# Low parts of weights and of gates made on GpSimd while the weights are decoded

## The chip, the cores and the metric

The kernel runs on one core of a Trainium2 chip. Its time is the device time of one execution in microseconds. TensorE is called PE here, VectorE DVE, ScalarE ACT, GpSimd POOL and SyncE SP, as in the profile.

## The reference

Four sequences of 768 tokens go through banded attention with eight heads, and the result through a layer of two matrix products with a gate between them:

```python
scores = scale * np.matmul(q, k.transpose(0, 1, 3, 2))   # then a bias by distance and a mask
a = np.exp(scores - max); a = a / (sum(a) + 1e-09)
x = np.matmul(a, v)                      # 3072 tokens x 512
h = x @ w_in                             # 512 -> 2048
g = h * np.clip(h + 3.0, 0.0, 6.0) / 6.0
out = g @ w_out                          # 2048 -> 512
```

The two weight matrices reach the kernel as 64-bit floats, seen as pairs of 32-bit words.

## The kernel before

The 3072 tokens are eight blocks of 384. For each block the kernel computes attention for four pairs of heads (which gives x) and then the two products. The 2048 inner columns are 16 *slices* of 128. For one slice `first` gives PE 12 matmuls of 384 columns into a bank hp, `gate` makes g from it (ACT, L185, then DVE, L186), and `second` gives PE 9 matmuls of 512 columns that add the slice's share to three banks acc. Each operand is split into a high part, rounded to the format that PE multiplies, and a low part, the rest; three of the four products of parts are added. So there are xh and xl, w1h and w1l, w2h and w2l, gh and gl. `high` makes gh, and `rest` makes gl = g - gh on DVE (L199), for which g has one buffer (`gp1`), gh four and gl three.

The weights come in 32 chunks of 128 x 512, w1 and w2 of a slice in turn, and `decode` makes them into 32-bit floats, high and low. For one chunk: SP loads the words (wst, three buffers); ACT takes the magnitude of the high word (wz, two buffers, L410) and makes the last places from the low word (we, L422; for the first six chunks POOL does this, L415); DVE clamps wz (L444) and shifts it (L445), puts the sign and exponent back (L453) and adds we (L457); ACT rounds to the high part (L461); and DVE subtracts to get the low part (L450), after which wz is free again.

The kernel begins with attention for the first nine pairs; the first three slices of block 0 lie beside it. Then come 21 *common slices*: block 0 (its remaining 13) and block 1 (its first 8) take turns as the digits of ORDER say, while the decode goes on beside them. Block 0 is the first to use a chunk throughout. After that the other slices of block 1 and all of blocks 2 to 7 run beside the attention of the block that follows. (At the end a flag chooses between storing the last block and a general path for other masks, which isn't taken here.)

`halves` lays out the common slices. For a slice it puts down `first`, the gate, gh (on ACT here) and gl, and then, with `finish`, the second product of the slice before. So a gl is used about one slice after its own gate.

How much of the decode is put between two slices is set by a plan when the program is written. `work(pe, dve)` adds the estimated costs of what was just put down to two sums, and as long as the sum of DVE is behind that of PE, `decode_step` takes the next quarter of a chunk from `decode`, which yields its estimated DVE cost: 0.68 for L444 and L445 of chunk i, 0.6 for the low part of chunk i-1, 0.6 for L453 of chunk i and 0.69 for L457. A slice counts 4.2 for PE (2.1 for each product) and 0.94 for DVE (0.47 for the gate, 0.47 for gl). `decoded_to` draws more steps where PE needs a chunk.

PE, POOL and SP work through their instructions in the order in which they are written (`in_order`). DVE and ACT get an order from the scheduler, which starts from the written one. Each engine serves its queue strictly in its order, and an instruction that waits holds up all that is behind it.

Of the kernel before, what the change touches and what calls it, by code (L numbers as in the profile page):

```python
# [9 lines left out]
F32 = mybir.dt.float32  # L10
# [4 lines left out]
ALU = mybir.AluOpType  # L15
# [38 lines left out]
WAKE = 9  # L54
FIRST = 3
CROWDED = 6
ORDER = "101001010010010100100"

def store(nc, pool, out, row, acc, last=False):
# [6 lines left out]
class Kernel:  # L66
# [127 lines left out]
            self.nc.scalar.copy(out=gh, in_=g)  # L194
        return gh

    def rest(self, g, gh):
        gl = self.lp.tile([P, TB], F32R, name="gl")
        self.nc.vector.tensor_tensor(out=gl, in0=g, in1=gh.bitcast(F32), op=ALU.subtract)  # L199
        return gl  # L200

    def second(self, f, acc, gh, gl, tiles=range(NT)):
# [201 lines left out]
    def magnitude(self, i):  # L404
# [6 lines left out]
        if i == 0:  # L411
            self.tc.add_manual_dep(self.nc.cur_bb.bb.instructions[-1], self.held, mybir.DependencyInfo(
                mybir.DependencyClass.NoSync, mybir.DependencyReason.DATA), reason="behind the first pairs")
        if i < CROWDED:
            self.nc.gpsimd.tensor_scalar(out=self.e[i], in0=words[:, :, 0].bitcast(U32), scalar1=2.0 ** -29, scalar2=0.0,  # L415
                                         op0=ALU.mult, op1=ALU.add)

    def last_places(self, i):
        if CROWDED <= i < 2 * NF:
            words = self.raw[i].rearrange("p (c w) -> p c w", w=2)  # L420
            before = self.nc.cur_bb.bb.instructions[-1].name
            self.nc.scalar.mul(out=self.e[i], in_=words[:, :, 0].bitcast(U32), mul=2.0 ** -29)  # L422
            self.tc.add_manual_dep(self.nc.cur_bb.bb.instructions[-1], before, mybir.DependencyInfo(
                mybir.DependencyClass.NoSync, mybir.DependencyReason.DATA), reason="behind the high part")
# [5 lines left out]
    def decode(self):  # L430

        nc = self.nc
        ts, stt, tt = nc.vector.tensor_scalar, nc.vector.scalar_tensor_tensor, nc.vector.tensor_tensor
        N = 2 * NF
        self.magnitude(0)
        for i in range(N + 1):
            a, b = i < N, i > 0
            if a:  # L440
                if i + 2 < N:
                    self.fetch(i + 2)
                z = self.z[i]
                ts(out=z.bitcast(F32), in0=z.bitcast(F32), scalar1=LEAST, scalar2=MOST, op0=ALU.max, op1=ALU.min)  # L444
                ts(out=z, in0=z, scalar1=0x07FFFFFF, scalar2=3, op0=ALU.bitwise_and, op1=ALU.logical_shift_left)  # L445
            yield 0.68 * a
            if b:
                hi, sh = self.part(i - 1, self.w1h, self.w2h)
                lo, _ = self.part(i - 1, self.w1l, self.w2l)
                tt(out=lo, in0=sh(self.z.pop(i - 1).bitcast(F32)), in1=hi.bitcast(F32), op=ALU.subtract)  # L450
            yield 0.6 * b
            if a:
                stt(out=z, in0=self.raw[i].rearrange("p (c w) -> p c w", w=2)[:, :, 1], scalar=-0x40000000, in1=z,  # L453
                    op0=ALU.bitwise_and, op1=ALU.bitwise_or)
            yield 0.6 * a
            if a:
                tt(out=z, in0=z, in1=self.e.pop(i), op=ALU.add)  # L457
                if i + 1 < N:
                    self.magnitude(i + 1)
                hi, sh = self.part(i, self.w1h, self.w2h)  # L460
                nc.scalar.copy(out=hi, in_=sh(z.bitcast(F32)))  # L461
                self.last_places(i + 1)
            yield 0.69 * a
# [16 lines left out]
        while self.decoded < 4 * (i + 1) + (2 if i < 2 * NF - 1 else 4):  # L480
            self.decode_step()

    def halves(self, steps, pool=False):


        for block, f, x, acc in steps:
            self.decoded_to(2 * f)
            g = self.gate(self.first(f, x), block == len(self.blocks) - 1 and f == NF - 1)
            gh = self.high(g, pool) if pool else None
            self.work(2.1, 0.47)  # L490
            yield
            if not pool:
                gh = self.high(g, pool)
            gl = self.rest(g, gh)
            self.work(0, 0.47)
            if self.last is not None:
                self.finish()
                yield
            self.last = (block, f, acc, gh, gl)
# [46 lines left out]
    def banded(self, flag):  # L546
# [12 lines left out]
        with ExitStack() as early, ExitStack() as words:  # L559
            x0 = self.x_tiles(self.pool("x0", 1, ctx=early, side="right"))  # L560
            xs = [x0, self.x_tiles(), self.x_tiles()]
            self.decoding(words, 3, 2, side="right")
            self.decoding_steps = self.decode()

            self.decoded_all = words.close
            self.fetch(0)
            self.given[1] = LEAD
            self.allowed = 4 * NF + 3
            acc = []
            with ExitStack() as ctx:  # L570
                self.load(2, False)
                self.fetch(1)
                for n in range(2):
                    self.load(n, True)
                self.plain_distances(ctx)
                self.attending(ctx, 9, 5)
                pairs = [Pair(self, n, xs[n // NPAIR], True) for n in range(EARLY)]
                todo = self.halves([(0, f, xs[0], acc) for f in range(FIRST)])

                def half():  # L580
                    if self.stage == "both":
                        next(todo, None)

                for n in range(-2, EARLY + 1):
                    if n + 2 < NPAIR:
                        self.distances(n + 2)
                    if n + 2 == EARLY:
                        self.stage = "both"
                        acc.extend(self.acc_tiles())
                    if n + 2 < EARLY:  # L590
                        weigh = []
                        for t in range(NT):
                            weigh.append(pairs[n + 2].scores(t))
                            if n == 0 and t < NT - 1:
                                self.spin(2)
                        if n < 0:
                            self.spin(5)
                        self.load_next(n + 2, False)
                        self.work(1.440, 0)
                    for t in range(NT):  # L600
                        if n + 2 < EARLY:
                            weigh[t]()
                            self.work(0, 0.64)
                            if t == NT - 1 and n == -2:
                                self.load(2, True)
                        if 0 <= n < EARLY:
                            pairs[n].turn(t)
                            if n == 0 and t < NT - 1:
                                self.spin(3)
                            self.work(0.396, 0)  # L610
                        if n + 1 in (0, 1):
                            pairs[n + 1].sum_up(t)
                            pairs[n + 1].normalize(t)
                        if t == 0:
                            if 2 <= n + 1 < EARLY:
                                pairs[n + 1].sum_up()
                            half()
                        if t == 1:
                            if n > 0:
                                pairs[n - 1].values()  # L620
                                self.work(1.350, 0.47)
                            if 2 <= n + 1 < EARLY:
                                for u in range(NT):
                                    pairs[n + 1].normalize(u)
                        if t == 2:
                            half()
                for _ in todo:
                    pass
            self.weights()
            self.packed_masks()  # L630
            self.allowed = 4 * (2 * NF + 1)
            acc1 = [pool.tile([P, BANK], F32, name=name) for pool, name in ((self.ps_s, "sp"), (self.ps_t, "tp"), (self.ps_x, "xp"))]
            self.given[1] = max(self.given)
            next_f, todo = [FIRST, 0], []
            for block in map(int, ORDER):
                todo.append((block, next_f[block], xs[block], (acc, acc1)[block]))
                next_f[block] += 1
            for _ in self.halves(todo):
                pass
            self.decoded_to(2 * NF - 1)  # L640
        self.attending(self.ctx, 3, 2, side="right")
# [13 lines left out]
        for i in range(2, len(self.blocks)):  # L655
# [7 lines left out]
            steps = [(i, f, x, acc) for f in range(NF)]  # L663
# [386 lines left out]
```

## Time and profile before

| | us |
|---|---|
| median of 3 runs (653.16 to 655.09) | 655.08 |
| the profiled execution | 654.68 |
| its span in the trace | 652.9 |
| PE busy in the span | 639.4 |
| DVE busy | 356.9 |
| ACT busy | 257.4 |
| POOL busy | 167.6 |

Times in the trace count from the start of the span. A group's row gives line, engine, operation, output and inputs with their shapes, how often it occurs, its busy time and the mean of one in ns, and behind the last bar the engine's idle time just before it and what ended most of that. In a timeline row the first two numbers are start and duration in us. Durations of one engine's neighbours overlap at their ends, so an engine's busy time is less than their sum. A row by stages gives the stretch, its length, the busy time of each engine, PE's granted clock, the share of the DMA engines and their GB/s.

### The profile page before, as it was taken

The numbers are of one execution on the slowest core, as the hardware profiler recorded it, in microseconds if no ns is written. First come the engines' busy times: TensorE is split into PE (matmuls) and PEld (weight loads), VectorE is DVE, ScalarE is ACT, GpSimd is POOL, SyncE is SP. The second block draws the span as 40 slices with busy tenths as digits, with TensorE's granted clock in tenths as the row PEclk, the third lists the DMA queues.
The fourth block names the chain that finished last, engine by engine and source line by source line (L and its number), as shares of the span: only waits on it lengthen the run. The fifth ranks groups of instructions, "written<-read, shape, count | busy, mean of one in ns | idle before, by whom it ended". The sixth has DMA issues, their size and how long they took to land.

```text
span 652.9 us, 13102 instructions
## 1 busy us (share of the span) xinstructions
PE 639.4 (98%) x4761; PEld 564.1 (86%) x4761; DVE 356.9 (55%) x1066; ACT 257.4 (39%) x706; POOL 167.6 (26%) x372
## 2 busy tenths in 40 slices
PE   8989999999999999999999999999999999999997
PEld 7778999997888889988898888888898888989985
DVE  5889999995644554255444454345542554422222
ACT  6897777775423222242313232132222423121111
POOL 5667000001422322034122332123220341202100
PEclk9999999999999999999999999999999999999999
DMA  7675644443565564346553455525643454310001
GB/s 281 182 238 194 189 157 149 143 129 113 126 189 169 147 192 125 90 118 165 164 134 102 117 154 163 141 78 154 184 126 89 122 136 122 94 43 8 1 0 54
DMA packets 47122, 86.23 MB, mean 132 GB/s; under 512 B 6504, under 2 KB 28872, under 8 KB 47048
## 3 DMA queue, kind: packets, MB, share of 16 engines
q1 hardware_dynamic: 46760, 85.03, 44.4%
q8 instruction: 40, 0.66, 0.4%
q14 instruction: 34, 0.28, 0.1%
q10 hardware_dynamic: 288, 0.26, 0.1%
HBM read 60.30 MB, written 24.97 MB: 131 GB/s over the span
## 4 chain that ended last, share of the span: by engine, by line
PE 83%; DVE 6%; ACT 4%; DMA 2%; POOL 2%; issue 2%; SPq 1%; POOLq 0%; ACTq 0%
PE hp L174 38%; PE acc L206 35%; ACT n L895 3%; PE xp L971 3%; PE sp L862 2%; PE sp L971 2%; DMA there<-blocks 1%; POOL n L915 1%; SPq L953 1%; DVE n L891 1%; PE xp L206 1%; PE tp L206 1%; PE sp L206 1%; DVE blocks L937 1%; DVE wz L453 1%
## 5 line engine op out<-in xcount | busy, mean ns | idle before, releaser
L185 ACT ACTIVATE g<-hp,small 128x384 f32<-128x384 f32 x127 | 73.6, 580 | 277.6 <-PE hp L174 173.4
L174 PE MATMUL hp<-xh,w1h 128*128 128x384 f32 x512 | 173.8, 340 | 0.5 <-ACT w1h L461 0.5
L174 PE MATMUL hp<-xh,w1l 128*128 128x384 f32 x512 | 172.3, 337 | 0.5 <-DVE w1l L450 0.5
L174 PE MATMUL hp<-xl,w1h 128*128 128x384 f32 x512 | 171.7, 335 | 0.0
L192 POOL TENSOR_SCALAR gh<-g 128x384 fp32r<-128x384 f32 x104 | 53.6, 515 | 343.6 <-DVE g L186 320.7
L186 DVE SCALAR_TENSOR_TENSOR g<-g,hp 128x384 f32<-128x384 f32 x128 | 70.7, 553 | 123.3 <-ACT g L185 122.1
L206 PE MATMUL acc<-w2h,gh 128*128 128x512 f32 x336 | 133.2, 396 | 0.0
L206 PE MATMUL acc<-w2h,gl 128*128 128x512 f32 x336 | 131.7, 392 | 0.0
L206 PE MATMUL acc<-w2l,gh 128*128 128x512 f32 x336 | 131.6, 392 | 0.0
L199 DVE TENSOR_TENSOR gl<-g,gh 128x384 fp32r<-128x384 f32 x128 | 71.5, 559 | 70.7 <-POOL gh L192 58.3
L895 ACT ACTIVATE n<-n,least 128x136 f32<-128x136 f32 (+2 forms) x192 | 79.5, 415 | 65.5 <-DVE least L891 64.8
L174 PEld LDWEIGHTS hp<-xh,w1h 128*128 128x128 f32 x512 | 96.1, 188 | 6.5 <-issue 3.1
L174 PEld LDWEIGHTS hp<-xl,w1h 128*128 128x128 f32 x512 | 96.2, 188 | 2.5
L174 PEld LDWEIGHTS hp<-xh,w1l 128*128 128x128 f32 x512 | 96.1, 188 | 1.1 <-DVE w1l L450 0.8
L915 POOL TENSOR_SCALAR n<-n,sums 128x136 f32<-128x136 f32 (+2 forms) x186 | 81.8, 457 | 38.3 <-DVE sums L906 23.1
L206 PEld LDWEIGHTS acc<-w2h,gh 128*128 128x128 f32 x336 | 63.1, 188 | 15.2 <-issue 3.3
L206 PEld LDWEIGHTS acc<-w2h,gl 128*128 128x128 f32 x336 | 63.1, 188 | 13.7 <-DVE gl L199 0.3
L206 PEld LDWEIGHTS acc<-w2l,gh 128*128 128x128 f32 x336 | 63.1, 188 | 11.4
L937 DVE STREAM_TRANSPOSE blocks<-n 128x256 f32<-128x256 f32 x138 | 51.1, 423 | 25.3 <-POOL n L915 20.8
L895 ACT ACTIVATION_READ_ACCUMULATOR n<-n,least 128x1 f32 x192 | 35.9, 187 | 0.0
L891 DVE CUSTOM_DVE_ANT_0 n<-sp,dl 128x136 f32<-128x136 f32 x60 | 17.7, 295 | 14.7 <-PE tp L862 14.7
L410 ACT ACTIVATE wz<-wst 128x512 f32<-128x512 f32 x32 | 21.5, 674 | 5.7 <-DVE w2l L450 2.8
(119 smaller groups left out, 644.6 us busy)
## 6 DMA issues: line engine op xcount, KB each, us to landing
there<-blocks SPq DMA_DIRECT2D x92, 192.0 KB
wst<-w SPq DMA_DIRECT2D x32, 512.0 KB
weights<-there SPq DMA_DIRECT2D x161, 96.0 KB
load<-pairs SPq DMA_DIRECT2D x31, 444.0 KB
load<-pairs SPq DMA_DIRECT2D x32, 384.0 KB
out<-o SPq DMA_DIRECT2D x23, 256.0 KB
weights<-there SPq DMA_DIRECT2D x23, 24.0 KB
there<-blocks SPq DMA_DIRECT2D x4, 72.0 KB
```

The lines of the kernel that those rows point to most:

```text
L174: self.nc.tensor.matmul(hp, lhsT=self.w1(w, f)[:, kt, :], rhs=a[:, kt, :], start=(n == 0), stop=(n == 3 * NKT - 1))
L185: nc.scalar.activation(out=g, in_=hp, func=AF.Relu, bias=self.three, scale=1.0)
L186: nc.vector.scalar_tensor_tensor(out=g, in0=g, scalar=6.0, in1=hp, op0=ALU.min, op1=ALU.mult)
L192: self.nc.gpsimd.tensor_scalar(out=gh, in0=g, scalar1=1.0, scalar2=0.0, op0=ALU.mult, op1=ALU.add)
L199: self.nc.vector.tensor_tensor(out=gl, in0=g, in1=gh.bitcast(F32), op=ALU.subtract)
L206: self.nc.tensor.matmul(acc[tt], lhsT=a[:, tk], rhs=self.w2(w, f), start=(f == 0 and j == 0), stop=(f == NF - 1 and j == 2))
L410: self.nc.scalar.activation(out=self.z[i].bitcast(F32), in_=words[:, :, 1].bitcast(F32), func=AF.Abs)
L891: nc.vector.tensor_tensor_reduce(out=e[:, j, lo:end], in0=sp[j][:, lo:end], in1=d, op0=ALU.add, op1=ALU.min, scale=scale, scalar=3.0e38, a ...
L895: nc.scalar.activation(out=e[:, j, lo:end], in_=e[:, j, lo:end], func=AF.Exp, bias=self.least[:, i:i + 1], scale=-1.0, accum_out=self.sums ...
L915: nc.gpsimd.tensor_scalar(out=e[:, j, lo:end], in0=e[:, j, lo:end], scalar1=over, scalar2=0.0, op0=ALU.mult, op1=ALU.add)
L937: nc.vector.transpose(out=self.blocks[:, :, s, t].rearrange("p b j q -> p j b q"), in_=e[:, :, c:c + P].rearrange("p j (b q) -> p j b q", ...
L971: nc.tensor.matmul(xps[j * D:(j + 1) * D, t * P:(t + 1) * P], lhsT=vt[0:K, t, j * D:(j + 1) * D], rhs=self.part(t, j, c, K), start=(c == 0 ...
```

## The change

Two kinds of subtractions move from DVE to POOL: the low part of weights of every chunk from the seventh on (26 of 32), and gl of the 21 common slices. Their costs in the plan become 0: the quarter with the low part yields 0 from `i = 7` on, and `work` is called with 0 instead of 0.47 after gl. POOL serves its queue in the written order.

```diff
+QUIET = 6
...
-    def rest(self, g, gh):
+    def rest(self, g, gh, pool=False):
         gl = self.lp.tile([P, TB], F32R, name="gl")
-        self.nc.vector.tensor_tensor(out=gl, in0=g, in1=gh.bitcast(F32), op=ALU.subtract)
+        (self.nc.gpsimd if pool else self.nc.vector).tensor_tensor(out=gl, in0=g, in1=gh.bitcast(F32), op=ALU.subtract)
...
-                tt(out=lo, in0=sh(self.z.pop(i - 1).bitcast(F32)), in1=hi.bitcast(F32), op=ALU.subtract)
-            yield 0.6 * b
+                (nc.gpsimd if i > QUIET else nc.vector).tensor_tensor(out=lo, in0=sh(self.z.pop(i - 1).bitcast(F32)),
+                                                                      in1=hi.bitcast(F32), op=ALU.subtract)
+            yield 0.6 * b * (i <= QUIET)
...
-    def halves(self, steps, pool=False):
+    def halves(self, steps, pool=False, low=False):
...
-            gl = self.rest(g, gh)
-            self.work(0, 0.47)
+            gl = self.rest(g, gh, low)
+            self.work(0, 0 if low else 0.47)
...
-            for _ in self.halves(todo):
+            for _ in self.halves(todo, low=True):
```

The plan's costs decide what lies between two slices, so the order of DVE, ACT and POOL changes; that of PE and of SP does not. On DVE, between the gates of the sixth and the seventh common slice (L186 g before, L187 after; wz is the chunk being decoded, w2l a low part), there stood:

```order
245 L186 SCALAR_TENSOR_TENSOR g<-g,hp 128x384
246 L445 TENSOR_SCALAR wz<-wz 128x512
247 L450 TENSOR_TENSOR w2l_147<-wz,w2h_146 128x512
248 L453 SCALAR_TENSOR_TENSOR wz<-wst,wz 128x512
249 L199 TENSOR_TENSOR gl<-g,gh 128x384
250 L457 ISA wz<-wz,we 128x1024
251 L444 TENSOR_SCALAR wz<-wz 128x512
252 L445 TENSOR_SCALAR wz<-wz 128x512
253 L186 SCALAR_TENSOR_TENSOR g<-g,hp 128x384
```

Now there stands between the same two gates, with line numbers one or two higher:

```order
238 L187 SCALAR_TENSOR_TENSOR g<-g,hp 128x384
239 L459 ISA wz<-wz,we 128x1024
240 L445 TENSOR_SCALAR wz<-wz 128x512
241 L446 TENSOR_SCALAR wz<-wz 128x512
242 L455 SCALAR_TENSOR_TENSOR wz<-wst,wz 128x512
243 L459 ISA wz<-wz,we 128x1024
244 L445 TENSOR_SCALAR wz<-wz 128x512
245 L446 TENSOR_SCALAR wz<-wz 128x512
246 L455 SCALAR_TENSOR_TENSOR wz<-wst,wz 128x512
247 L187 SCALAR_TENSOR_TENSOR g<-g,hp 128x384
```

The low part of weights and gl are gone, and instead of five decode operations there are eight, those of two chunks.

On POOL, behind the last masks that are prepared for later attention (dl) and ahead of what the second attention stage needs (blocks, load), there stood nothing:

```order
45 L298 TENSOR_SCALAR dl<-d_85 32x128
46 L298 TENSOR_SCALAR dl<-d_86 32x136
47 L306 MEMSET blocks 128x3x192
48 L848 TENSOR_SCALAR load_72<-load_72,over 128x384
49 L192 TENSOR_SCALAR gh<-g 128x384
```

Now the queue goes on at that place as follows:

```order
45 L299 TENSOR_SCALAR dl<-d_85 32x128
46 L299 TENSOR_SCALAR dl<-d_86 32x136
47 L200 TENSOR_TENSOR gl<-g,gh 128x384
48 L451 TENSOR_TENSOR w1l_145<-wz,w1h_144 128x4x128
49 L451 TENSOR_TENSOR w2l_147<-wz,w2h_146 128x512
50 L200 TENSOR_TENSOR gl<-g,gh 128x384
51 L451 TENSOR_TENSOR w1l_145<-wz,w1h_144 128x4x128
52 L451 TENSOR_TENSOR w2l_147<-wz,w2h_146 128x512
53 L200 TENSOR_TENSOR gl<-g,gh 128x384
```

Two low parts of weights lie between two gl. The end of this piece of the queue is

```order
84 L451 TENSOR_TENSOR w1l_1025<-wz,w1h_1024 128x4x128
85 L200 TENSOR_TENSOR gl<-g,gh 128x384
86 L451 TENSOR_TENSOR w2l_1027<-wz,w2h_1026 128x512
87 L200 TENSOR_TENSOR gl<-g,gh 128x384 x7
88 L307 MEMSET blocks 128x3x192
```

so that the last low part stands between the fourteenth and the fifteenth gl, and seven gl follow it; blocks and what is behind it come after all of them.

## The prediction

> **What bounds the kernel now.** I read the page's busy shares and slices first, then the busy times of the stretch that the change touches, then PE's timeline there, and then the groups of that stretch by shape.
>
> ```profile
> PE 639.4 (98%) x4761; PEld 564.1 (86%) x4761; DVE 356.9 (55%) x1066; ACT 257.4 (39%) x706; POOL 167.6 (26%) x372
> ## 2 busy tenths in 40 slices
> PE   8989999999999999999999999999999999999997
> DVE  5889999995644554255444454345542554422222
> ACT  6897777775423222242313232132222423121111
> POOL 5667000001422322034122332123220341202100
> ```
>
> The span is 652.9 us, and PE is busy in 98% of it, so whatever does not make PE wait is free, and whatever does is paid in full. One of these slices is 16.3 us. From the fifth to the tenth DVE stands at 9 while POOL stands at 0: that is the stretch of the common slices, in which the weights are decoded beside the first two blocks, and the change moves work there from the one engine to the other.
>
> ```profile
> 64.00:146.00 82.00, 82.00 (x425) 74.51 (x422) 78.98 (x160) 62.96 (x111) 0.00 (x0) 1.00 0.49 153
> 146.00:160.00 14.00, 13.04 (x106) 10.80 (x106) 8.28 (x19) 7.21 (x13) 2.65 (x4) 1.00 0.25 70
> ...
> 149.04 0.44 PE L174 MATMUL hp<-xh,w1h 128*128 128x384 f32 x1 [0.47 <-ACT w1h L461]
> 150.13 0.44 PE L174 MATMUL hp<-xh,w1l 128*128 128x384 f32 x1 [0.48 <-DVE w1l L450]
> ```
>
> The columns are PE, PEld, DVE, ACT and POOL busy. DVE works 78.98 of 82.00 us, yet PE loses nothing before 146. It waits twice, 0.47 and 0.48 us, where the last hidden slice's weights come late. So a relieved DVE can give back 0.95 us here and no more: this bounds the gain.
>
> **The change, part by part.** These are the groups of the same 82 us by shape, first DVE's.
>
> ```profile
> L453 DVE SCALAR_TENSOR_TENSOR wz<-wst,wz 128x512 int32<-128x512 int32 x24 | 16.5, 686 | 0.0
> L457 DVE CUSTOM_DVE_ANT_0 wz<-wz,we 128x1024 uint16<-128x1024 uint16 x24 | 16.5, 686 | 0.4
> L199 DVE TENSOR_TENSOR gl<-g,gh 128x384 fp32r<-128x384 f32 x20 | 11.1, 553 | 0.0
> L186 DVE SCALAR_TENSOR_TENSOR g<-g,hp 128x384 f32<-128x384 f32 x19 | 10.5, 551 | 2.4 <-ACT g L185 2.2
> L445 DVE TENSOR_SCALAR wz<-wz 128x512 int32<-128x512 int32 x24 | 10.1, 423 | 0.2
> L444 DVE TENSOR_SCALAR wz<-wz 128x512 f32<-128x512 f32 x24 | 10.1, 421 | 0.0
> L450 DVE TENSOR_TENSOR w1l<-wz,w1h 128x512 fp32r<-128x512 f32 x12 | 8.2, 686 | 0.0
> L450 DVE TENSOR_TENSOR w2l<-wz,w2h 128x512 fp32r<-128x512 f32 x12 | 8.2, 686 | 0.0
> L161 DVE TENSOR_TENSOR xl<-xp,xh 128x384 fp32r<-128x384 f32 x1 | 0.5, 545 | 0.0
> ```
>
> *What leaves DVE.* The busy times add up to 91.7 us against the 78.98 of the whole engine: neighbours overlap at their ends, and a duration counts for 0.861 of itself. A chunk without its low part is 421 + 423 + 686 + 686 = 2216 ns, so 1.91 us of DVE; a gate (L186) is 0.47 us; each low part of weights that leaves frees 0.59, each gl 0.48.
>
> *What POOL pays.* The trace has no large two-input operation on POOL. The nearest rows are these.
>
> ```profile
> L192 POOL TENSOR_SCALAR gh<-g 128x384 fp32r<-128x384 f32 x104 | 53.6, 515 | 343.6 <-DVE g L186 320.7 <-PE acc L206 16.5 <-ACT xh L160 4.0
> L1034 POOL MEMSET const-float32-0.0<- 128x1 f32 x1 | 0.1, 100 | 0.2 <-issue 0.2
> ...
> 54.20 0.66 POOL L415 TENSOR_SCALAR we<-wst 128x512 int32<-128x512 uint32 x1
> 55.54 1.00 POOL L415 TENSOR_SCALAR we<-wst 128x512 int32<-128x512 uint32 x1 [0.68 <-DVE wz L453]
> ...
> 54.26 1.14 DVE L453 SCALAR_TENSOR_TENSOR wz<-wst,wz 128x512 int32<-128x512 int32 x1
> 55.93 1.15 DVE L457 CUSTOM_DVE_ANT_0 wz<-wz,we 128x1024 uint16<-128x1024 uint16 x1
> ```
>
> With one input POOL takes 0.66 us for 512 columns and 0.52 for 384, of which 0.10 is there with one column. That is the lower end. Two inputs read one after the other double what is left: 0.10 + 2 x 0.56 = 1.21 us and 0.10 + 2 x 0.415 = 0.93 us, the upper end. I take the upper, because 1.1 ns per column and input is what POOL's rows show at both widths, and nothing in them suggests a second input for free. [...]
>
> *What the two engines do to each other.* The last four rows decide the forecast. L453 needs 0.69 us when POOL is idle. Beside the POOL operation of 54.20 to 54.86 it takes 1.14 and ends 0.54 us after POOL does. L457 beside 55.54 to 56.54 takes 1.15 and ends again 0.54 us after; and that POOL operation itself took 1.00, not 0.66, because it began while L453 still ran. So these DVE operations and POOL's take turns. By the rows, time on POOL is time taken from DVE, and the move brings no parallel work except beside the gate, which reads one of its inputs from the matmul's banks. [...]
>
> *What the order does.* The planner now counts nothing on DVE for the moved work, so each slice draws two chunks where it drew one or two (1.9 against 1.3 by its own costs). The rows of the change's section show two full decodes between two gates on DVE, and a gl, two low parts, a gl on POOL. All queues are served in order. So a gl, for which PE waits, now stands behind two low parts on POOL; its gate stands behind two decodes on DVE; the next slice's ACT operation waits for gl, since g has one buffer; and a chunk's first step waits for the low part two chunks before, since wz has two. The order of PE and of SP's transfers stays as it was.
>
> ```profile
> 70.25 0.55 DVE L199 TENSOR_TENSOR gl<-g,gh 128x384 fp32r<-128x384 f32 x1
> ...
> 123.56 0.56 DVE L199 TENSOR_TENSOR gl<-g,gh 128x384 fp32r<-128x384 f32 x1
> ...
> 125.87 0.39 PE L206 MATMUL sp<-w2h,gl 128*128 128x512 f32 x1
> ```
>
> *The sum.* POOL's queue now has 13 gl and 25 low parts from the first common slice's gl up to the fourteenth's; then one low part and seven gl are left. Before, these two gl start at 70.25 and 123.56: 53.3 us, 4.1 us a slice. In turns, the same stretch costs
>
> - DVE: 25 chunks x 1.91 = 47.7 us
> - POOL, low parts of weights: 25 x 1.21 = 30.3 us
> - POOL, gl: 13 x 0.93 = 12.1 us
> - the gates, 13 x 0.47 = 6.1 us, half of them beside POOL: 3.1 us
>
> together 93.2 us, 7.2 a slice, 39.9 more than before. PE takes the fourteenth gl at 125.87, 1.75 us after it is made (124.12), so the first 1.75 us are hidden; and the 0.95 us of late weights go, because the decode now ends seven slices early. Net: 39.9 - 1.75 - 0.95 = 37.2 us. From the fifteenth slice on PE runs at its old pace, as all that follows does: it is only shifted. The profiled execution took 654.68 us (span 652.9 and 1.8 around it), the median of the three timed runs is 655.08, within 0.1%. Forecast: 654.7 + 37.2 = 692 us. Its own range: 0.54 instead of 0.59 us a turn for the long DVE operations, and likewise the short ones, takes off 25 x 0.17 = 4 us; gates wholly hidden or not at all, 3 either way: 685 to 695, and up to 698 where handing over costs 0.1 us for some 30 turns.
>
> **The rivals.**
>
> *Turns and chain together (slower still).* With two wz buffers, a chunk's steps follow each other at their full durations, 2.22 instead of 1.91 us, and nothing hides the gate (0.55): 25 x (2.22 + 1.21) + 13 x (0.93 + 0.55) = 104.9 us, net +48.9, so 704 us. For it: DVE's order has the four steps of a chunk in a row. Against it: POOL can use the gaps. PE could reach the same place by its clock:
>
> ```profile
> 32.00:48.00 16.00, 13.29 (x139) 11.13 (x138) 14.21 (x59) 15.23 (x51) 10.22 (x21) 1.00 0.71 230
> ...
> 44.31 0.44 PE L971 MATMUL xp<-pt,load 128*64 128x128 f32 x4 [1.42 <-issue]
> ```
>
> PE waits 1.42 us here, more than anywhere between the first pairs and the end, with the granted clock at 1.00 (the column after POOL's); the forecast has about 3 us a slice. At half clock a slice would need 8.2 us, more than 7.2: 13 x 8.2 - 53.3 - 2.7 = +50.6, 705 us. [...]
>
> *POOL cheap.* A two-input operation costs what one input does: 47.7 + 25 x 0.66 + 13 x 0.52 + 3.1 = 74.1 us, net +18.1: 673 us. For it: only that the trace has no such row. Against it: 1.1 ns per column at both widths.
>
> *Side by side (not slower).* POOL's two-input operations do not take turns with DVE's. Then POOL needs 2 x 1.21 + 0.93 = 3.35 us a slice, less than PE's 4.1; DVE needs 47.7 + 6.1 = 53.8 us for the stretch, as PE's 53.3; and the next limit is ACT:
>
> ```profile
> L422 ACT ACTIVATE we<-wst 128x512 int32<-128x512 uint32 x24 | 16.2, 674 | 0.0
> L410 ACT ACTIVATE wz<-wst 128x512 f32<-128x512 f32 x23 | 15.5, 673 | 3.5 <-DVE w1l L450 1.6 <-DVE w2l L450 1.2
> L185 ACT ACTIVATE g<-hp,small 128x384 f32<-128x384 f32 x19 | 11.0, 580 | 8.5 <-PE hp L174 7.4 <-DVE wz L457 0.9
> L194 ACT CAST gh<-g 128x384 fp32r<-128x384 f32 x20 | 10.2, 511 | 2.2 <-DVE g L186 1.8
> L461 ACT CAST w2h<-wz 128x512 fp32r<-128x512 f32 x12 | 7.5, 623 | 3.5 <-DVE wz L457 3.0
> L461 ACT CAST w1h<-wz 128x512 fp32r<-128x512 f32 x12 | 7.4, 621 | 1.3 <-DVE wz L457 0.6
> L160 ACT CAST xh<-xp 128x384 fp32r<-128x384 f32 x1 | 0.5, 472 | 0.0
> ```
>
> These add up to 68.3 us against 62.96 busy, a factor of 0.92. 25 chunks at (674 + 673 + 623) x 0.92 = 1.81 us and 13 gates at (580 + 511) x 0.92 = 1.00 us make 58.3, net 58.3 - 53.3 - 2.7 = +2.3: 657 us; if ACT packs closer, the whole gain stays: 653.7. So this rival ends at 654 to 657, and it decides as soon as a slice's two decodes and gl fit in PE's 4.1 us. The four rows of turns speak against it; they are one-input POOL operations, and so it keeps a chance. Since PE waits for nothing else that this change reaches, more than 0.95 us cannot come off.
>
> **How the numbers follow.** A measurement of this kernel tells 0.3%, 2 us, from no change. Forecast 0.68; 704 or 705, 0.09; POOL cheap 0.11; side by side 0.12. Of the last, 0.08 lies within 2 us, 0.02 above, and 0.02 goes to faster, for a wait that I do not see. Slower is 0.68 + 0.09 + 0.11 + 0.02 = 0.90. The range goes from 669, below the cheap rival by the 4 us of the shorter turns, to 704. It leaves out the side-by-side case and about half of the slowest: under 2 in 10.
>
> **What would show it.** Right: between 70 and 165 us PE waits about 3 us a slice, mostly for POOL's gl; POOL's low parts of weights take 1.2 us or more and gl 0.9 or more; L453 and L457 (now L455 and L459) are longer than 686 ns where POOL is busy; DVE and POOL busy together add up to the stretch; the last low part is made near 160, with seven slices to come; after that the slices have their 4.1 us again. Wrong: the decode operations at 686 ns beside a busy POOL (side by side); POOL's wide one at 0.66 us (cheap); PEclk below 1 in the stretch, or DVE and POOL both idle while PE waits (the slower case).

## The result, and the profile after

The changed kernel takes 693.93 us (median of 4 runs, 693.38 to 697.32) against 654.88 before: 1.061 times as long, with a 95% interval of 1.057 to 1.065, or 39 us more. The forecast was 692 us, in a range from 669 to 704. The profiled execution took 693.55 us, its span 691.7.

The page after, the rows that answer to those of before:

```profile
PE 653.5 (94%) x4761; PEld 571.8 (83%) x4761; DVE 364.5 (53%) x1019; ACT 258.2 (37%) x706; POOL 226.4 (33%) x419
## 2 busy tenths in 40 slices
PE   8989868768999999999999999999999999999997
DVE  5888599996145255434544455425544454523212
ACT  6897466564243243213331323214331322212111
POOL 5664454555243033213322233203312232212100
PEclk9999988998999999999999999999999999999999
```

One of these slices is now 17.3 us. Between the fifth and the tenth, where PE stood at 9, it stands at 6 to 8. POOL's zeros are gone, and DVE, which gave away 47 operations, is busy for 364.5 us, 7.6 more than before: its operations last longer than they did. PE's granted clock falls too, to a mean of 0.98 from 1.00, and PE is busy 653.5 us with the same 4761 matmuls that took 639.4.

The groups between 64 and 165 us by shape show which operations grew:

```profile
L455 DVE SCALAR_TENSOR_TENSOR wz<-wst,wz 128x512 int32<-128x512 int32 x25 | 35.8, 1431 | 0.8
L459 DVE CUSTOM_DVE_ANT_0 wz<-wz,we 128x1024 uint16<-128x1024 uint16 x25 | 23.5, 938 | 1.7 <-ACT we L423 0.2
L200 POOL TENSOR_TENSOR gl<-g,gh 128x384 fp32r<-128x384 f32 x14 | 18.4, 1314 | 16.0 <-issue 8.1 <-ACT gh L195 8.0
L451 POOL TENSOR_TENSOR w1l<-wz,w1h 128x512 fp32r<-128x512 f32 x13 | 17.4, 1337 | 19.6 <-ACT w1h L463 19.6
L451 POOL TENSOR_TENSOR w2l<-wz,w2h 128x512 fp32r<-128x512 f32 x12 | 16.3, 1361 | 17.2 <-ACT w2h L463 17.2
```

L455 (L453 before) went from 686 to 1431 ns, L459 (L457) from 686 to 938. The rows count an operation that is held up as busy for as long as it waits. One slice of the timeline shows how, POOL's operations first, then DVE's:

```profile
99.24 1.44 POOL L200 TENSOR_TENSOR gl<-g,gh 128x384 fp32r<-128x384 f32 x1
101.97 1.27 POOL L451 TENSOR_TENSOR w1l<-wz,w1h 128x512 fp32r<-128x512 f32 x1 [1.29 <-ACT w1h L463]
105.59 1.28 POOL L451 TENSOR_TENSOR w2l<-wz,w2h 128x512 fp32r<-128x512 f32 x1 [2.35 <-ACT w2h L463]
106.83 1.45 POOL L200 TENSOR_TENSOR gl<-g,gh 128x384 fp32r<-128x384 f32 x1
...
99.97 1.27 DVE L459 CUSTOM_DVE_ANT_0 wz<-wz,we 128x1024 uint16<-128x1024 uint16 x1
102.06 1.73 DVE L455 SCALAR_TENSOR_TENSOR wz<-wst,wz 128x512 int32<-128x512 int32 x1
103.72 0.54 DVE L187 SCALAR_TENSOR_TENSOR g<-g,hp 128x384 f32<-128x384 f32 x1
104.18 0.68 DVE L459 CUSTOM_DVE_ANT_0 wz<-wz,we 128x1024 uint16<-128x1024 uint16 x1
105.69 1.73 DVE L455 SCALAR_TENSOR_TENSOR wz<-wst,wz 128x512 int32<-128x512 int32 x1
```

POOL's w1l runs from 101.97 to 103.24. L455 starts 0.09 us behind it and ends at 103.79, again 0.55 us after POOL. L459, at 104.18 with POOL idle, takes its 0.68. From one gl to the next pass 7.59 us, where PE needs 4.1.

The start of the stretch, and the fourteenth gl on POOL with PE's next use of it:

```profile
64.38 0.62 ACT L463 CAST w1h<-wz 128x512 fp32r<-128x512 f32 x1
...
70.23 0.99 POOL L200 TENSOR_TENSOR gl<-g,gh 128x384 fp32r<-128x384 f32 x1 [8.09 <-issue]
71.18 1.26 POOL L451 TENSOR_TENSOR w1l<-wz,w1h 128x512 fp32r<-128x512 f32 x1
...
72.50 0.66 PE L175 MATMUL hp<-xh,w1l 128*128 128x384 f32 x1 [3.04 <-POOL w1l L451]
...
164.97 1.45 POOL L200 TENSOR_TENSOR gl<-g,gh 128x384 fp32r<-128x384 f32 x1
...
166.47 0.50 PE L207 MATMUL sp<-w2h,gl 128*128 128x512 f32 x1 [0.49 <-POOL gl L200]
```

The two gl stand 94.7 us apart; 53.3 before, 93.2 by the forecast. At the start of the stretch the order of POOL's queue costs time by itself: the high part of w1 was ready at 65.00 and POOL idle, but w1l is written behind the first gl, and PE waited 3.04 us for it. And these are PE's longest waits between 64 and 170 us (total, number of times, longest):

```profile
PE acc L207 <- POOL gl L200: 12.4, 7, 2.7
PE sp L207 <- POOL gl L200: 6.7, 4, 4.2
PE hp L175 <- POOL w1l L451: 4.3, 2, 3.0
```

### The profile page after: what moved, and what is told of

Read it like the earlier page. It is cut to its first block, busy times and chain, and to the rows that moved or that the text cites. A ratio compares the mean times of both kernels' runs of the same rounds, so it can differ in the third digit from the quotient of the medians.

```text
span 691.7 us, 13114 instructions
## 1 busy us (share of the span) xinstructions
PE 653.5 (94%) x4761; PEld 571.8 (83%) x4761; DVE 364.5 (53%) x1019; ACT 258.2 (37%) x706; POOL 226.4 (33%) x419
## 4 chain that ended last, share of the span: by engine, by line
PE 75%; DVE 14%; issue 4%; POOL 3%; ACT 2%; DMA 1%; SPq 0%; DVEq 0%; POOLq 0%; ACTq 0%
PE hp L175 34%; PE acc L207 31%; DVE wz L455 5%; DVE wz L459 3%; PE xp L973 2%; PE sp L864 2%; PE sp L973 2%; DVE wz L446 2%; DVE wz L445 1%; ACT n L897 1%; PE sp L207 1%; PE tp L207 1%; POOL n L917 1%; PE xp L207 1%; DVE n L893 1%
## 5 line engine op out<-in xcount | busy, mean ns | idle before, releaser
L186 ACT ACTIVATE g<-hp,small 128x384 f32<-128x384 f32 x127 | 73.4, 578 | 283.2 <-PE hp L175 184.6
L175 PE MATMUL hp<-xh,w1l 128*128 128x384 f32 x512 | 174.7, 341 | 4.3 <-POOL w1l L451 4.3
L175 PE MATMUL hp<-xh,w1h 128*128 128x384 f32 x512 | 176.3, 344 | 0.2 <-ACT w1h L463 0.2
L175 PE MATMUL hp<-xl,w1h 128*128 128x384 f32 x512 | 174.0, 340 | 0.0
L193 POOL TENSOR_SCALAR gh<-g 128x384 fp32r<-128x384 f32 x104 | 53.3, 512 | 339.4 <-DVE g L187 318.6
L187 DVE SCALAR_TENSOR_TENSOR g<-g,hp 128x384 f32<-128x384 f32 x128 | 70.7, 552 | 148.4 <-ACT g L186 147.4
L207 PE MATMUL acc<-w2h,gl 128*128 128x512 f32 x336 | 134.4, 400 | 12.5 <-POOL gl L200 12.4
L207 PE MATMUL acc<-w2h,gh 128*128 128x512 f32 x336 | 135.0, 402 | 1.6 <-ACT gh L195 1.5
L175 PEld LDWEIGHTS hp<-xh,w1h 128*128 128x128 f32 x512 | 98.3, 192 | 6.5 <-issue 3.1
L175 PEld LDWEIGHTS hp<-xl,w1h 128*128 128x128 f32 x512 | 98.1, 192 | 2.7
L200 DVE TENSOR_TENSOR gl<-g,gh 128x384 fp32r<-128x384 f32 x107 | 59.8, 559 | 69.8 <-POOL gh L193 58.0
L455 DVE SCALAR_TENSOR_TENSOR wz<-wst,wz 128x512 int32<-128x512 int32 x32 | 41.1, 1285 | 0.8
L200 POOL TENSOR_TENSOR gl<-g,gh 128x384 fp32r<-128x384 f32 x21 | 25.5, 1213 | 34.2 <-ACT gh L195 22.9
```

What stands on the lines that cost most here:

```text
L175: self.nc.tensor.matmul(hp, lhsT=self.w1(w, f)[:, kt, :], rhs=a[:, kt, :], start=(n == 0), stop=(n == 3 * NKT - 1))
L186: nc.scalar.activation(out=g, in_=hp, func=AF.Relu, bias=self.three, scale=1.0)
L187: nc.vector.scalar_tensor_tensor(out=g, in0=g, scalar=6.0, in1=hp, op0=ALU.min, op1=ALU.mult)
L193: self.nc.gpsimd.tensor_scalar(out=gh, in0=g, scalar1=1.0, scalar2=0.0, op0=ALU.mult, op1=ALU.add)
L200: (self.nc.gpsimd if pool else self.nc.vector).tensor_tensor(out=gl, in0=g, in1=gh.bitcast(F32), op=ALU.subtract)
L207: self.nc.tensor.matmul(acc[tt], lhsT=a[:, tk], rhs=self.w2(w, f), start=(f == 0 and j == 0), stop=(f == NF - 1 and j == 2))
```

## The experiments

The theory was *turns*: an operation of POOL that reads and one of DVE that needs two inputs exclude each other, and so do a reading one of POOL and the one-input operations of the decode (L444 and L445, 0.42 us for 512 columns where two inputs take 0.69). The expectations call the shorter time of one-input operations the double-rate mode: in the trace of before two inputs take 553 ns for 384 columns (L199) and 686 for 512 (L450), so 1.04 ns a column, and another one-input operation on DVE (L913) takes 282 for 128 and 335 for 232, so about 0.51. Its rivals were *order* (decodes queued ahead of gates cost the time by themselves), *chain* (the two wz buffers set the pace) and *side by side*. All times below stand against runs of the kernel before on the same chip.

**POOL reads beside the kernel before.** The order of DVE and ACT in the stretch stays, and DVE keeps all its work; what POOL computes goes into a spare tile (o) and is thrown away.

```diff
+    def beside(self, a):
...
+        ts.tensor_tensor(out=o, in0=a.bitcast(F32), in1=a.bitcast(F32), op=ALU.subtract)
...
+                if i > 6:
+                    self.beside(hi)
...
+            if low:
+                self.beside(gh)
```

> The kernel before, with all its work and its plan where it was, and beside it POOL subtracts two equal inputs into a spare tile: 512 columns once for each chunk from the seventh on, 384 columns once for each common slice. Nobody waits for the results. Turns: DVE gets no relief and loses 25 x 1.27 + 21 x 1.00 = 53 us of time to POOL, about 5 of them beside gates and 3 in its idle time: 40 to 45 us slower, 690 to 700; L453, L457, L450 and L199 last well over 0.69 and 0.55 us where POOL works. Side by side, or order: 655, since no order and no dependence changes.

Measured: 686.68 us against 654.73, ratio 1.048 (1.045 to 1.050), 32 us slower. Nothing waits for this work and the order stayed, so the two engines do take turns. The expectation was 690 to 700 us; the size was missed by 8 to 13 us. DVE's operations between 64 and 185 us show where the time went (gl took 553 ns before, L465 and L461 686, L451 423):

```profile
L205 DVE TENSOR_TENSOR gl<-g,gh 128x384 fp32r<-128x384 f32 x21 | 23.1, 1098 | 0.0
L465 DVE CUSTOM_DVE_ANT_0 wz<-wz,we 128x1024 uint16<-128x1024 uint16 x26 | 22.8, 875 | 0.5
L451 DVE TENSOR_SCALAR wz<-wz 128x512 int32<-128x512 int32 x25 | 20.4, 814 | 0.2
L461 DVE SCALAR_TENSOR_TENSOR wz<-wst,wz 128x512 int32<-128x512 int32 x25 | 20.0, 798 | 0.0
```

L451 has one input, so POOL's reads hold up such operations too.

**POOL writes beside the kernel before.** A one-column operation (one is the first column of a) stays, so that POOL has the same inputs to wait for. Against the run above:

```diff
-        ts.tensor_tensor(out=o, in0=a.bitcast(F32), in1=a.bitcast(F32), op=ALU.subtract)
+        ts.tensor_scalar(out=self.spare[:, 0:1], in0=one.bitcast(F32), ...)
+        for _ in range(2):
+            ts.memset(o, 0.0)
```

> As the run with POOL's extra subtractions, but POOL fills the spare tile with zeros instead, twice for each of them, behind a one-column operation that keeps the pace: about as long on POOL (0.6 us for each filling of 512 columns), with almost nothing read. Turns between reads only: L453, L457, L450 and L199 keep 0.69 and 0.55 us, and only the operations with one input in the double-rate mode (L444, L445) may be held up by a write, 0.2 to 0.3 us a chunk: 655 to 662. Turns with anything that POOL does: 40 us slower, as the run with subtractions. Side by side: 655.

Measured: 655.03 us against 654.73, ratio 1.000 (0.999 to 1.001). Between 64 and 146 us POOL works for 56 us beside a DVE as full as before. The first row is that stretch (PE, PEld, DVE, ACT and POOL busy), the others are groups of it:

```profile
64.00:146.00 82.00, 81.86 (x422) 74.14 (x419) 79.73 (x159) 62.87 (x111) 56.01 (x126) 1.00 0.49 153
...
L204 POOL MEMSET spare<- 128x512 f32 x46 | 25.4, 552 | 2.7
L468 DVE CUSTOM_DVE_ANT_0 wz<-wz,we 128x1024 uint16<-128x1024 uint16 x24 | 16.4, 683 | 0.4
L464 DVE SCALAR_TENSOR_TENSOR wz<-wst,wz 128x512 int32<-128x512 int32 x23 | 15.6, 680 | 0.0
L454 DVE TENSOR_SCALAR wz<-wz 128x512 int32<-128x512 int32 x24 | 11.2, 467 | 0.2
L453 DVE TENSOR_SCALAR wz<-wz 128x512 f32<-128x512 f32 x24 | 10.6, 440 | 0.0
```

The two-input operations keep 683 and 680 ns (686 before); only those with one input rise, from 423 and 421 to 467 and 440, which is 0.06 us a chunk where 0.2 to 0.3 were expected. So beside the kernel before, POOL's being busy costs next to nothing: its reads do.

**The change with the plan's old costs.**

```diff
-            yield 0.6 * b * (i <= QUIET)
+            yield 0.6 * b
...
-            self.work(0, 0 if low else 0.47)
+            self.work(0, 0.47)
```

> POOL makes the same low parts as in the change, but the plan keeps its old costs (0.6 for a low part of weights, 0.47 for a gl), so the decode is spread over all 21 common slices. Turns (theory: an operation of POOL that reads and one of DVE with two inputs take turns): 25 chunks x (1.91 + 1.27) + 20 slices x (1.00 + 0.24) = 104.3 us from the first common gl to the last, where it was 83.8; less 2.7 for slack and late weights, so about 18 us over the kernel before: 673 us, between 666 and 680. Order (rival: the loss comes from two decodes being queued ahead of each gate, not from turns): 655 to 660, as POOL has room for its work beside DVE. In both the decode operations show which it is: 1.2 us and more beside POOL, or 0.69.

Measured: 698.29 us against 654.73, ratio 1.067 (1.063 to 1.070). Neither theory gave this. PE's waits between 66 and 190 us, and POOL's, are now others:

```profile
POOL gl L200 <- ACT gh L195: 35.6, 15, 6.1
PE hp L175 <- POOL w1l L451: 13.6, 5, 3.4
```

PE waits in its first product for a w1l, and POOL waits in its queue for a gh. One of the five waits, with the two operations of POOL before it:

```profile
89.14 0.99 POOL L200 TENSOR_TENSOR gl<-g,gh 128x384 fp32r<-128x384 f32 x1 [3.51 <-ACT gh L195]
90.09 1.44 POOL L451 TENSOR_TENSOR w1l<-wz,w1h 128x512 fp32r<-128x512 f32 x1
...
91.59 0.69 PE L175 MATMUL hp<-xh,w1l 128*128 128x384 f32 x1 [3.37 <-POOL w1l L451]
```

In that queue the low part stood behind the gl of the slice before; gl waits for its gate, and the gate for PE. So now and then a ring closes over POOL and PE, which the sum by turns (673 us) does not have. That became a theory, and the next run its test.

**The same, with the decode laid out two chunks ahead.**

```diff
-            self.given[1] = max(self.given)
+            self.given[1] = max(self.given) - 5.2
```

> The run with the old costs took 698 us, where turns alone had given 673. In it POOL's queue puts the low part that PE's next slice needs behind a gl that has to wait for the gate of the slice before. Here the plan starts two chunks ahead, so that each low part stands two places earlier against the gl. Ring (theory: POOL's queue and PE wait for each other in turn): the extra 25 us go for the most part, 670 to 682. Turns alone, or something else in DVE's work: 694 or more, as the work is the same.

Measured: 676.84 us against 655.71, ratio 1.031 (1.029 to 1.033): 22 us less over before than the run above. PE's waits for w1l, 13.6 us there, are gone; that the rest of the 22 belongs to the ring as well is argued, not shown, as the order of DVE and ACT changed with the plan. POOL's row now reads

```profile
POOL gl L200 <- ACT gh L195: 24.4, 12, 3.6
```

What is left, 21 us over before, is near the 18 of turns alone. Of all kernels here that make all these low parts on POOL this is the fastest.

**The plan's costs alone, all work on DVE.**

```diff
-                (nc.gpsimd if i > QUIET else nc.vector).tensor_tensor(out=lo, ...)
+                nc.vector.tensor_tensor(out=lo, ...)
...
-            gl = self.rest(g, gh, low)
+            gl = self.rest(g, gh)
```

> Only the plan's costs change (0 for the low parts from the seventh chunk on and for gl); all work stays on DVE. If the plan by itself put two decodes between two gates on DVE, DVE would fall behind its gates: 25 x 2.50 + 13 x 0.95 = 74.9 us for 13 slices of 53.3, 670 us or more. If DVE's order comes from the scheduler, which goes by what it takes DVE to be free for, nothing changes: 655.

Measured: 654.74 us against 654.82, ratio 1.000 (0.999 to 1.002). With the work on DVE the zeros do nothing: the order of its gates and decode operations is that of before. With the work on POOL they do something, since the changed kernel and the run with the old costs differ in the zeros alone: POOL's queue is another, and so is DVE's order, with mostly eight decode operations between two gates where the old costs leave mostly four. The zeros made it 4 us faster there (694 for 698).

**The change with three wz buffers.**

```diff
-        self.zp = self.pool("zp", bufs, ctx=ctx, **kw)
+        self.zp = self.pool("zp", bufs + (bufs == 2), ctx=ctx, **kw)
```

> The changed kernel with three buffers wz instead of two, so that the magnitude of a chunk need not wait for POOL's low part two chunks before. Turns: the sum of DVE's and POOL's work stays, so 690 to 694. Chain (rival: the steps of a chunk behind each other, through two buffers, set the pace): a third chunk in flight takes 10 us or more off, 684 or less.

Measured: 692.23 us against 654.73, ratio 1.058 (1.055 to 1.061). A third chunk in flight hardly moves it, so the buffers were not the pace.

**The change without POOL's reads, POOL's queue unchanged.** Of each low part that the change moved POOL subtracts one column only, and then it fills the whole tile twice with zeros; so this kernel leaves these low parts out.

```diff
+    def fill(self, out, a, b, one):
...
+        self.nc.gpsimd.tensor_tensor(out=one(out), in0=one(a), in1=one(b), op=ALU.subtract)
+        for _ in range(2):
+            self.nc.gpsimd.memset(out.bitcast(F32), 0.0)
...
+        if pool:
+            self.fill(gl, g, gh.bitcast(F32), lambda a: a[:, 0:1])
...
+                if i > QUIET:
+                    self.fill(lo, low_z, hi.bitcast(F32), ...)
```

> The changed kernel with its queues, waits and plan, but POOL subtracts only the first column of each low part and then fills the tile twice with zeros (0.55 to 0.6 us each for 512 columns, 0.48 for 384), so it works as long and reads almost nothing. It leaves out the low parts that the change moved: they are zero. Turns: the decode operations are back at 0.69 us, the stretch of 13 slices runs at the pace of PE or ACT: 654 to 660. Order (rival: that gates and gl stand behind two decodes in queues that are served in order costs the time by itself): 685 or more.

Measured: 670.88 us against 655.71, ratio 1.023 (1.022 to 1.025): 15 us over before, where the change is 39 over. So about 24 us go with the reads, and 15 do not, which neither expectation had. In the groups between 70 and 145 us the two-input operations of the decode are back at their old length, but those with one input are not (423 and 421 before):

```profile
L471 DVE CUSTOM_DVE_ANT_0 wz<-wz,we 128x1024 uint16<-128x1024 uint16 x24 | 16.6, 692 | 3.6 <-ACT we L432 0.9
L467 DVE SCALAR_TENSOR_TENSOR wz<-wst,wz 128x512 int32<-128x512 int32 x24 | 16.5, 688 | 0.6
L455 DVE TENSOR_SCALAR wz<-wz 128x512 int32<-128x512 int32 x24 | 12.3, 512 | 0.6
L454 DVE TENSOR_SCALAR wz<-wz 128x512 f32<-128x512 f32 x24 | 12.2, 508 | 6.0 <-ACT wz L420 6.0
```

So the fillings still hold DVE up a little. And POOL's queue is that of the changed kernel, but the scheduler gave DVE and ACT another order: on DVE the gate now mostly stands behind a one-input operation of the decode, and in the changed kernel mostly behind the one that puts the sign back (L455 there). The split into 24 and 15 is therefore rough.

**The same with one filling instead of two.** The edit is `for _ in range(2)` taken out above.

> The run without reads took 671 us, 15 more than the kernel before. Here POOL fills each tile once instead of twice, so its work falls by nearly half, with the same queues; the low parts that the change moved are again zero. Order (theory: what is left of the loss is that two decodes are queued ahead of each gate): 666 to 671. POOL's sheer time (rival: about 4 us a slice for POOL, near PE's 4.1): 660 or less.

Measured: 664.16 us against 654.82, ratio 1.015 (1.012 to 1.019). It fell between the two: of the 15 us about 6 go with half of POOL's fillings, and 9 stay with POOL's queue as it is and the other half. The decode's one-input operations fell to 440 and 424 ns between 70 and 145 us, so part of the 6 us may be that fillings no longer hold them up, and not POOL's time; this was not separated. Of the 9 us one piece can be named: PE still waits 2.2 us for the first w1l behind the first gl (3.0 in the changed kernel, 3.3 with two fillings).

**Both taken away.** The decode two chunks ahead with the old costs, and POOL's reads replaced by two fillings as above.

> Both causes taken away at once: the queues of the run with chunks two places earlier (677 us), and POOL reads one column and fills the tile twice with zeros, as in the run without reads (671 us). It leaves out the low parts that the change moved: they are zero. Turns and order: with neither left, PE sets the pace again, 654 to 658. If a third cause is at work (POOL's sheer time, or ACT's), it stays at 662 or more.

Measured: 659.82 us against 654.82, ratio 1.007 (1.006 to 1.009). Against the run with the same queue on POOL and with reads (21 us over before) 16 us go, so reads are the larger part here too. The last 5 us lie between the two bounds that were set, and what they are was not tried.

**One half of the change at a time.** For the first run only `self.halves(todo, low=True)` goes back to `self.halves(todo)`; for the second, the low parts of weights stay on DVE at 0.6.

> Only the low parts of weights are on POOL; gl stays on DVE. Turns: about 1.5 chunks a slice, so 16 slices with the whole decode: 25 x 3.18 + 16 x (0.48 + 0.24) = 91.0 us where it was 16 x 4.1 = 65.6; less 2.7: 23 us slower, 678, between 670 and 684. Side by side: 654 to 657.

Measured: 680.24 us against 655.71, ratio 1.038 (1.036 to 1.039): 24.5 us slower, where 23 were expected.

> Only gl is on POOL; the low parts of weights stay on DVE. Turns: about 1.4 chunks a slice, 18 slices: 25 x 2.50 + 18 x (1.00 + 0.24) = 84.8 us where it was 73.8; less 2.7: 8 us slower, 663, between 658 and 668. Side by side: DVE is relieved by 10 us and PE's 0.95 us of waits go: 654.

Measured: 659.28 us against 655.71, ratio 1.007 (1.004 to 1.009): 3.6 us slower, where 8 were expected. So each half loses alone, in the order of its time on POOL, and together they lose 11 us more than the sum of both.

## Why the prediction was right

- **The bound** (0.95 us to be won): not contradicted, and not tested by itself. No run here is below the kernel before by more than a measurement can tell, but each that relieves DVE also gives POOL work beside it.
- **POOL's price** (1.21 and 0.93 us): right, the upper end. Operations that were not held up took 1.27 and 1.28, and 0.99 us, in the rows above; with those that had to wait for DVE the means are 1.34 and 1.36, and 1.31. So the rival with a cheap POOL (673 us) falls.
- **Turns**: right, and shown. Reads beside an unchanged DVE cost 32 us, writes 0.3. The 0.54 us read off two rows of before came again as 0.55.
- **One reading**: the wrong operation, though the same behaviour. POOL's 1.00 us from 55.54 on did not begin while L453 ran, which ended at 55.40, but while L450 did, a two-input operation as well, and ended 0.53 us after it. The row of before:

```profile
55.33 0.68 DVE L450 TENSOR_TENSOR w2l<-wz,w2h 128x512 fp32r<-128x512 f32 x1
```

- **The stretch of 13 slices** (93.2 us): 94.7. PE now takes the fourteenth gl as soon as it is made, so the slack of 1.75 us was given back; that gl itself took longer (1.45 for 0.56), and the late weights went: the span grew by 38.8 us, for 37.2.
- **How it was put together**: only partly right, and that the sum came out this close is in part luck. The sum charged all 39.9 us to turns, with the gates as the only work beside POOL. A gate does run beside it: the one at 81.41 took its 0.56 us wholly beside a w1l that took 1.29, from 80.72 on. But half of the gates were counted so, and of the 13 in the stretch this was the only one; two more overlap by 0.07 us. In the run without reads 24 of 39 us go with the reads; of the rest, about 6 go with half of POOL's fillings, and 9 stay. In the real stretch there are waits of POOL for ACT's high part (19.6 and 17.2 us in the groups above) which the sum lacks. DVE is not full throughout either: between 70 and 84 us it works 6.80 of 14.00 us. The sum also lacks what made up for this: in the experiment that added reads, turns at 1.27 and 1.00 us gave 40 to 45 us and 32 were measured.
- **The signs**: PE was to wait about 3 us a slice; it waits 24 us in the 13 slices, 1.9 a slice, and is busy for 70.68 us where it was 53.31, at a mean granted clock of 0.87. DVE and POOL busy were to add up to the stretch; they add up to 133.8 us (83.76 and 50.02) for 94.7, for the most part because waiting for the other engine counts as busy.
- **The plan**: right only together with the move. "Each slice draws two chunks" is true of POOL's queue and, with the work on POOL, of DVE's order; the zeros alone change nothing.
- **Side by side, 654 to 657 us**: as a rival rightly given little, but its price left out the queues. With the reads gone and POOL's queue kept it is 671.
- **Turns and chain** (704 us): not so. A third wz buffer brings 1.7 us.
- **The clock**: it did fall, as the first rival said it might, and the prediction named this among the signs of the slower case; but it did not set the pace. No run shows the 705 us that the prediction reckons with half clock throughout: the granted clock stood at 0.50 in pieces of the stretch only, as from 100 to 106 us, and at 0.87 over all of it, and 694 us were measured. These two rows are two neighbouring slices of the changed kernel (the granted clock stands behind POOL's count):

```profile
99.00:106.50 7.50, 5.76 (x16) 5.09 (x17) 7.23 (x10) 4.79 (x8) 3.87 (x4) 0.56 0.46 135
106.50:114.00 7.50, 6.11 (x28) 4.62 (x26) 7.23 (x10) 4.72 (x8) 3.87 (x4) 0.99 0.48 145
```

At 0.56 and at 0.99 DVE is busy for the same 7.23 us of 7.50, and the gl at 99.24, 106.83 and 114.43 stand equally far apart (7.59 and 7.60 us). What the lower clock may have cost at the end of the stretch was not tried.

## What to carry to other kernels

Before work is moved from DVE to POOL, look in the trace for places where both already run at once. Here DVE operations with two inputs ended a fixed time after POOL's operation did (0.54 us), the two took turns, and POOL's time was DVE's (reads beside an unchanged DVE cost 32 us). Then 0.59 us off DVE for 1.27 on POOL was a loss on a full DVE, whatever POOL's idle time said: 24.5 us with the low parts of weights alone. On a queue that is served in written order, also ask what each moved instruction waits for and who stands behind it: with low parts behind a gl that waits for PE, the same work took 22 us more than when it was written two chunks earlier.

## What the runs showed that was not expected

POOL's writes were nearly free beside a full DVE: 56 us of work in 82 us, most of it fillings, for 0.3 us of time. Only the decode's one-input operations grew beside them (423 to 467 and 421 to 440 ns). PE's granted clock fell to 0.56 over a stretch in which PE still worked three quarters of the time (5.76 of 7.50 us); its longest wait there is this one:

```profile
100.74 0.80 PE L207 MATMUL acc<-w2h,gl 128*128 128x512 f32 x1 [2.72 <-POOL gl L200]
```
